# Gated linear attention into an FFN on one core: the FFN's activation, the weights' low parts and the order of the program rewritten

## The chip, the cores and the metric

One core of a Trainium2 chip runs the whole program in one launch. The metric is the device time of an execution in microseconds (us). The engines of a core run side by side, each in the order of its own queue: PE (TensorE, matrix products into PSUM banks), DVE (VectorE), ACT (ScalarE), POOL (GpSimd) and SP (SyncE, which here only issues DMAs). They wait for each other by semaphores.

## What is computed

```python
for t in range(S):                                   # B=4, H=8, S=768, D=48
    state = alpha[:, :, t, :, None] * state + einsum('bhd,bhe->bhde', k[:, :, t], v[:, :, t])
    y[:, :, t] = einsum('bhd,bhde->bhe', q[:, :, t], state)
x = y.transpose(0, 2, 1, 3).reshape(3072, 384)
h = x @ w_in                                         # w_in 384 x 2048
g = where(h >= 1, h, where(h <= -1, 0, (h + 1)**2 / 4))
out = (g @ w_out).astype(float32)                    # w_out 2048 x 384
```

The attention's inputs are float32. The weights are float64 (8 bytes a number) in device memory and are turned into fp32 on the chip.

## The kernel before, in words

**Chunks.** The sequence is cut into 24 chunks of 128 tokens, six to a batch entry. `prepare` (lines 452 to 529) loads a chunk and makes its running products of alpha: two scans on DVE (L498 forward, L505 backward, a reciprocal L502 between them), the product with the keys (L513, DVE) and with the queries (L526, POOL). `attend` (777 to 804) turns it: PE transposes (L545), scores (L560) and the state's update (L573), DVE masks the scores (L646) and adds to the state (L600, L602), ACT or POOL copy the state for PE (L592, L595), and PE makes the outputs (L700). `end_chunk` (726 to 774) brings the outputs into the layout of the FFN: for the first three chunks one fp32 copy on ACT (L738); for later ones a rounded part on ACT (L747) and the rest by DVE's subtraction (L752) in a ring, and behind the last chunk of a group six small DMAs of SP (L768) that move pieces between partitions.

**Groups.** Three chunks are a group of 384 tokens, eight groups in all. Each group runs over 16 blocks of 128 columns of w_in ("f-blocks"): a first product (x by w_in) into a PSUM bank h, the activation, a second product (g by w_out) added up in three PSUM banks over the 16 blocks. In group 0 both are plain fp32 products (L819 and L920). From group 1 on each number is split into a rounded high part and a low part and a product is three products of parts, 9 matmuls (L828, "split" first product; L929, split second product). For that g is split too: the high part by ACT (L894), the low part by POOL or DVE (L895). The last f-block's sums are copied by ACT or DVE (L332) and sent out (L968).

**Activation before** (lines 861 to 890): DVE clips h to -1..1 into gf (L876), ACT makes (0.5 gf + 0.5) squared (L861), DVE takes the maximum with h (L887). For f-blocks with a key under CLIPS = 6 (the first five of group 0) ACT makes three operations instead of DVE's clip: Relu(-0.5 h + 0.5) out of PSUM, Relu(1 - that), Square.

**Weights.** Two f-blocks share one tile of w_in and one of w_out ("wt", 128 x 768 float64, 768 KB), 16 tiles in all. `decode` (340 to 399) makes fp32 of a tile: ACT (L350, L358), DVE shift (L366), DVE sign (L377), and an integer addition (L389) that POOL or DVE makes. Group 0 uses the decoded tiles as they are. For group 1 and later, `part_w` (401 to 415) makes the rounded high part on ACT (L404) and the low part by a subtraction on POOL or, as the other way, DVE (L405).

**The order.** Nothing is written in program order: every operation is handed to a `Plan` (75 to 226) with an engine, an assumed time, a key (roughly the time at which it is due) and what it reads and writes. `Plan.order` then goes through the program on the host and puts on each engine's queue, one after the other, what can start soonest by the assumed times, the smallest key first. An operation may name a second engine ("other"), which then counts LATER later. The constants in lines 31 to 51 set the keys: LAG is by how many f-blocks the second product follows the first, FETCH, LOAD, DECODE and PARTED how far ahead the weights are fetched, decoded and split, PREPARE and the MARGINs how far ahead chunks are made ready, MERGE from which chunk on a group's f-blocks are planned together with the next chunk. RATE is the assumed rate of a DMA. Where PE would idle for long at the beginning, matmuls of zeros are put in ("fills", L980).

Of the kernel before, what the change touches and what calls it, by code (L numbers as in the profile page):

```python
# [14 lines left out]
AF = mybir.ActivationFunctionType  # L15
ALU = mybir.AluOpType
# [14 lines left out]
LAG = 3.0  # L31
FETCH = 12.0
LOAD = 6.0
DECODE = 3.0
PARTED = 6.0
PREPARE = 2.5
MARGIN = 11.0
MARGIN0 = 9.0
MARGIN1 = 6.0
FETCH0 = 18.0  # L40
DECODE0 = 4.0
AHEAD = 20.0
FIRST = 5
ROOM = 2
LATER = 4.0
MERGE = 6
WARMTH = 60.0
HELP = 4
QFAST = 3
CLIPS = 6.0  # L50
# [24 lines left out]
class Plan:  # L75
# [6 lines left out]
    ISSUE, LAND, RATE = 0.42, 1.9, 190e3  # L82
# [50 lines left out]
    def order(self):  # L133
        free = {"PE": 1.0, "DVE": 1.0, "ACT": 1.0, "POOL": 5.0, "SP": 1.0}
# [95 lines left out]
def gated_attention_ffn(ctx: ExitStack, tc: tile.TileContext, q, k, v, alpha, w_in, w_out, by, out):  # L230
    nc = tc.nc
# [20 lines left out]
        out=mask, in_=mask, compare_op=ALU.is_ge, fill=0.0, base=0, pattern=[[1, P]], channel_multiplier=-1  # L252
# [53 lines left out]
    with ExitStack() as main:  # L306
# [33 lines left out]
        def decode(u, which, raw, key):  # L340
# [7 lines left out]
                0.88,  # L348
# [7 lines left out]
                0.87,  # L356
# [35 lines left out]
                1.82,  # L392
# [414 lines left out]
        def hidden(n, f, key):  # L807
# [57 lines left out]
            if key < CLIPS:  # L865


                act(h, AF.Relu, -0.5, half_b)
                act(gf, AF.Relu, -1.0, ones)
                act(gf, AF.Square, 1.0, 0.0)  # L870
            else:
                plan.op(
                    "DVE",
                    0.08 + 0.45 * w,
                    key + 0.4,
                    lambda: nc.vector.tensor_scalar(  # L876
                        out=gf(), in0=h(), scalar1=-1.0, scalar2=1.0, op0=ALU.max, op1=ALU.min
                    ),
                    [h],
                    [gf],  # L880
                )
                act(gf, AF.Square, 0.5, half_b)
# [4 lines left out]
                lambda: nc.vector.tensor_tensor(out=gf(), in0=gf(), in1=h(), op=ALU.max),  # L887
# [307 lines left out]
```

## Time and profile before

| | |
|---|---|
| runs | median 545.0 us (544.95 to 545.48, 3 runs) |
| the profiled execution | 543.69 us, of which its span in the trace 541.4 us |
| granted clock of PE, mean | 0.986 |
| PE busy | 517.4 us, 96% |
| DVE, ACT, POOL busy | 381.7, 251.9, 171.8 us: 70%, 47%, 32% |

Shares of busy time are means over the span. The slices of the page show where an engine is full and where it is not; the releaser of an idle time is the instruction whose end let the waiting one start. A duration in a row is that of the instruction on its engine, with what it lost there to others.

### The profile page before, as it was taken

The numbers are of one execution on the slowest core, as the hardware profiler recorded it, in microseconds if no ns is written. First come the engines' busy times: TensorE is split into PE (matmuls) and PEld (weight loads), VectorE is DVE, ScalarE is ACT, GpSimd is POOL, SyncE is SP. The second block draws the span as 40 slices with busy tenths as digits, with TensorE's granted clock in tenths as the row PEclk, the third lists the DMA queues.
The fourth block names the chain that finished last, engine by engine and source line by source line (L and its number), as shares of the span: only waits on it lengthen the run. The fifth ranks groups of instructions, "written<-read, shape, count | busy, mean of one in ns | idle before, by whom it ended". The sixth has DMA issues, their size and how long they took to land.

```text
span 541.4 us, 11717 instructions
## 1 busy us (share of the span) xinstructions
PE 517.4 (96%) x4753; PEld 471.5 (87%) x4753; DVE 381.7 (70%) x637; ACT 251.9 (47%) x455; POOL 171.8 (32%) x180
## 2 busy tenths in 40 slices
PE   7998979788999999999999999999999999999996
PEld 5875545456999999999999999999999999999995
DVE  6688988989976587577687677667677656555553
ACT  2578847544444444444444444444444444334331
POOL 5746677666541232042122322133114300000000
PEclk8999998999999999999999999999999999999999
DMA  7998350716421232042123132033202011001001
GB/s 183 281 327 259 124 158 0 234 35 157 126 84 57 50 113 84 16 106 81 49 83 86 39 110 84 16 91 110 78 6 58 21 45 24 1 1 45 0 1 48
DMA packets 22330, 46.98 MB, mean 87 GB/s; under 512 B 3616, under 2 KB 11776, under 8 KB 22272
## 3 DMA queue, kind: packets, MB, share of 16 engines
q1 hardware_dynamic: 22272, 46.18, 29.5%
q8 instruction: 39, 0.64, 0.5%
q14 instruction: 19, 0.16, 0.1%
HBM read 39.38 MB, written 4.72 MB: 81 GB/s over the span
## 4 chain that ended last, share of the span: by engine, by line
PE 86%; DVE 5%; DMA 3%; issue 2%; POOL 2%; SPq 0%; ACT 0%; POOLq 0%; DVEq 0%; ACTq 0%
PE ps L828 33%; PE ps L929 33%; PE ps L700 5%; PE ps L920 4%; PE ps L819 3%; PE ps L573 2%; PE ps L560 2%; PE ps L545 2%; PE ps L980 2%; DMA both<-in_vb 1%; DVE w L377 1%; DVE inv L505 1%; POOL wt L389 1%; DMA wt<-in_w_out 1%; DMA raw_kq<-in_kq 1%
## 5 line engine op out<-in xcount | busy, mean ns | idle before, releaser
L828 PE MATMUL ps<-ring,wt 128*128 128x384 f32 x1008 | 197.4, 340 | 0.0
L929 PE MATMUL ps<-gh,wt 128*128 128x384 f32 x1008 | 197.4, 340 | 0.0
L828 PEld LDWEIGHTS ps<-ring,wt 128*128 128x128 f32 x1008 | 178.0, 188 | 1.1
L929 PEld LDWEIGHTS ps<-gh,wt 128*128 128x128 f32 x1008 | 177.3, 188 | 0.6 <-issue 0.2
L861 ACT ACTIVATE gf<-gf,half_b 128x384 f32<-128x384 f32 x123 | 76.0, 618 | 136.2 <-DVE gf L876 134.9
L887 DVE TENSOR_TENSOR gf<-gf,ps 128x384 f32<-128x384 f32 x128 | 70.3, 550 | 59.4 <-ACT gf L861 58.5
L894 ACT CAST gh<-gf 128x384 fp32r<-128x384 f32 x112 | 57.5, 513 | 72.7 <-DVE gf L887 69.3
L876 DVE TENSOR_SCALAR gf<-ps 128x384 f32<-128x384 f32 x123 | 68.2, 554 | 24.8 <-PE ps L828 18.3
L895 POOL TENSOR_TENSOR gh<-gf,gh 128x384 fp32r<-128x384 f32 x38 | 41.5, 1092 | 103.7 <-ACT gh L894 88.7
L895 DVE TENSOR_TENSOR gh<-gf,gh 128x384 fp32r<-128x384 f32 x74 | 42.8, 578 | 41.8 <-ACT gh L894 41.8
L526 POOL TENSOR_TENSOR Q<-pre,raw_kq 128x512 f32<-128x512 f32 x24 | 31.6, 1315 | 127.4 <-PE ps L700 117.0
L920 PE MATMUL ps<-gf,wt 128*128 128x384 f32 x96 | 37.3, 535 | 6.1 <-POOL wt L389 4.9
L405 POOL TENSOR_TENSOR wt<-wt 128x768 fp32r<-128x768 f32 x15 | 33.6, 2244 | 13.8 <-ACT wt L404 13.6
L920 PEld LDWEIGHTS ps<-gf,wt 128*128 128x128 f32 x96 | 19.7, 212 | 19.1 <-POOL wt L389 5.8
L498 DVE TENSOR_TENSOR_SCAN pre<-raw_a,fwd 128x516 f32<-128x516 f32 x24 | 31.4, 1309 | 5.2 <-POOL fwd L273 2.1
L819 PE MATMUL ps<-wt 128*128 128x384 f32 x96 | 33.0, 491 | 1.9 <-POOL wt L389 1.9
L505 DVE TENSOR_TENSOR_SCAN inv<-raw_a,bwd 128x516 f32<-128x516 f32 x24 | 31.9, 1331 | 0.3
L819 PEld LDWEIGHTS ps<-wt 128*128 128x128 f32 x96 | 18.5, 196 | 14.2 <-POOL wt L389 2.8
L592 ACT COPY both<-state 48x192 f32<-48x192 f32 x69 | 24.0, 348 | 11.7 <-POOL state L677 5.3
L548 ACT COPY ks<-ps 128x512 f32<-128x512 f32 x24 | 14.1, 588 | 28.8 <-PE ps L545 28.7
L700 PE MATMUL ps<-other,both 128*64 128x64 f32 x372 | 27.0, 226 | 0.0
L700 PE MATMUL ps<-Q,both 128*64 128x64 f32 x372 | 26.9, 226 | 0.0
(69 smaller groups left out, 494.6 us busy)
## 6 DMA issues: line engine op xcount, KB each, us to landing
raw_kq<-in_kq SPq DMA_DIRECT2D x48, 192.0 KB, 3.8
raw_a<-in_al SPq DMA_DIRECT2D x24, 258.5 KB, 2.6
both<-in_vb SPq DMA_DIRECT2D x48, 128.0 KB, 2.8
wt<-in_w_in SPq DMA_DIRECT2D x8, 768.0 KB, 8.8
wt<-in_w_out SPq DMA_DIRECT2D x8, 768.0 KB, 5.4
vt<-in_vt SPq DMA_DIRECT2D x24, 192.0 KB, 3.2
out<-ot SPq DMA_DIRECT2D x24, 192.0 KB, 1.9
ring<-ring SPq DMA_DIRECT2D x42, 48.0 KB, 2.2
```

Of the source, the lines that this page charges most:

```text
L405: sub = lambda e: e.tensor_tensor(out=part(1), in0=data(), in1=part(0).bitcast(F32), op=ALU.subtract)
L505: lambda: nc.vector.tensor_tensor_scan(flat(inv())[:, ::-1], a[:, 1 : n + 1][:, ::-1], flat(bwd)[:, ::-1], 0.0, ALU.mult, ALU.max),
L700: nc.tensor.matmul(out=ps()[halves[r], to, halves[u]], lhsT=lhsT[:, u, r], rhs=x()[:, g, halves[u]], start=m + u == 0, stop=True, skip_gro ...
L819: nc.tensor.matmul(out=h(), lhsT=raw_in(f)[:, kt], rhs=whole_x(n)()[:, kt].rearrange("p j t -> p (j t)"), start=kt == 0, stop=kt == KT - 1,)
L828: nc.tensor.matmul(out=h(), lhsT=win(f, w)[:, kt], rhs=ring[:, at, kt, a, :], start=(m == 0), stop=(m == 3 * KT - 1),)
L861: lambda: nc.scalar.activation(out=gf(), in_=in_(), func=func, scale=scale, bias=bias),
L876: lambda: nc.vector.tensor_scalar(out=gf(), in0=h(), scalar1=-1.0, scalar2=1.0, op0=ALU.max, op1=ALU.min),
L887: lambda: nc.vector.tensor_tensor(out=gf(), in0=gf(), in1=h(), op=ALU.max),
L894: plan.op("ACT", 0.08 + 0.41 * w, key + 0.4, lambda: nc.scalar.copy(out=gh()[:, 0], in_=gf()), [gf], [gh])
L895: sub = lambda e: e.tensor_tensor(out=gh()[:, 1], in0=gf(), in1=gh()[:, 0].bitcast(F32), op=ALU.subtract)
L920: nc.tensor.matmul(out=o_ps[seg][m](), lhsT=raw_out(f)[:, m * P : (m + 1) * P], rhs=gh(), start=f == f0, stop=f == f1 - 1,)
L929: nc.tensor.matmul(out=o_ps[seg][m](), lhsT=wout(f, w)[:, m * P : (m + 1) * P], rhs=gh()[:, a], start=(f == f0 and i == 0), stop=(f == f1 ...
```

## The change

The activation becomes two operations on ACT, r = Relu(0.5 h + 0.5) out of PSUM and r squared, and one on DVE, max(min(r squared, 1), h), for all f-blocks alike; the clip on DVE (L876), the maximum (L887) and the three-operation form go, and CLIPS with them. The low part of the weights is made by DVE alone. The constants of the plan, some of its assumed times, its assumed DMA rate and the engines' assumed first free times are others, so the order is made anew on all engines. Line numbers of the new file are smaller by one to 25.

```diff
-LAG = 3.0   FETCH = 12.0  LOAD = 6.0   DECODE = 3.0   PARTED = 6.0   PREPARE = 2.5
-MARGIN = 11.0  MARGIN0 = 9.0  MARGIN1 = 6.0  FETCH0 = 18.0  DECODE0 = 4.0  AHEAD = 20.0
-FIRST = 5   ROOM = 2  LATER = 4.0  MERGE = 6  HELP = 4  QFAST = 3  CLIPS = 6.0
+LAG = 5     FETCH = 9     LOAD = 11.0  DECODE = 12.5  PARTED = 10.5  PREPARE = 3.5
+MARGIN = 9.0   MARGIN0 = 9.5  MARGIN1 = 5.5  FETCH0 = 22    DECODE0 = 2.0  AHEAD = 8
+FIRST = 4   ROOM = 3  LATER = 5.0  MERGE = 3  HELP = 7  QFAST = 16
-    ISSUE, LAND, RATE = 0.42, 1.9, 190e3
+    ISSUE, LAND, RATE = 0.42, 1.9, 280e3
-        free = {"PE": 1.0, "DVE": 1.0, "ACT": 1.0, "POOL": 5.0, "SP": 1.0}
+        free = {"PE": 2.5, "DVE": 2.5, "ACT": 2.5, "POOL": 6.0, "SP": 2.8}
...
-                1.82,
+                1.95,
-                other=("DVE", 1.55, lambda: add(nc.vector), True),
+                other=("DVE", 0.96, lambda: add(nc.vector), True),
...
-            plan.op(
-                "POOL",
-                1.8,
-                key,
-                lambda: sub(nc.gpsimd),
-                [raw, parts],
-                [parts],
-                port=True,
-                other=("DVE", 0.88, lambda: sub(nc.vector), True),
-            )
+            plan.op("DVE", 0.88, key, lambda: sub(nc.vector), [raw, parts], [parts], port=True)
...
-            if key < CLIPS:
-                act(h, AF.Relu, -0.5, half_b)
-                act(gf, AF.Relu, -1.0, ones)
-                act(gf, AF.Square, 1.0, 0.0)
-            else:
-                plan.op("DVE", ..., lambda: nc.vector.tensor_scalar(
-                        out=gf(), in0=h(), scalar1=-1.0, scalar2=1.0, op0=ALU.max, op1=ALU.min), [h], [gf])
-                act(gf, AF.Square, 0.5, half_b)
+            act(h, AF.Relu, 0.5, half_b)
+            act(gf, AF.Square, 1.0, 0.0)
             plan.op("DVE", ...,
-                lambda: nc.vector.tensor_tensor(out=gf(), in0=gf(), in1=h(), op=ALU.max),
+                lambda: nc.vector.scalar_tensor_tensor(
+                    out=gf(), in0=gf(), scalar=1.0, in1=h(), op0=ALU.min, op1=ALU.max),
                 [gf, h], [gf])
```

(The constants are set several to a line here, and three statements are drawn together.)

Counts on the queues, before and after: fills on PE 159 and 98; L876 on DVE 123 and none; the low part of the weights on DVE 1 and 16, on POOL 15 and none; the low part of g on DVE 74 and 86, on POOL 38 and 26; ACT's activations 138 and 256.

**DVE at the start**, behind the product of chunk 0. "pre", "bwd" and "inv" are a chunk's scans, reciprocal and product with the keys; "Q" is masked scores. Before:

```order
L498 SCALAR_TENSOR_TENSOR pre<-raw_a,fwd 128x516
L646 TENSOR_TENSOR Q<-ps,mask 64x4x64 x2
L600 COPY state<-ps 128x192
L502 RECIPROCAL bwd<-pre 128x4
L602 TENSOR_TENSOR state<-state,ps 128x192
L505 SCALAR_TENSOR_TENSOR inv<-raw_a,bwd 128x516
L513 TENSOR_TENSOR inv<-inv,raw_kq 128x4x128
L646 TENSOR_TENSOR Q<-ps,mask 64x4x64 x2
```

and with the change (L488, L492, L495, L503 are the lines that were L498, L502, L505, L513; L636, L590 and L592 were L646, L600 and L602):

```order
L488 SCALAR_TENSOR_TENSOR pre<-raw_a,fwd 128x516
L492 RECIPROCAL bwd<-pre 128x4
L495 SCALAR_TENSOR_TENSOR inv<-raw_a,bwd 128x516
L503 TENSOR_TENSOR inv<-inv,raw_kq 128x4x128
L636 TENSOR_TENSOR Q<-ps,mask 64x4x64 x2
L590 COPY state<-ps 128x192
L592 TENSOR_TENSOR state<-state,ps 128x192
L636 TENSOR_TENSOR Q<-ps,mask 64x4x64 x2
```

Chunk 1's scans, reciprocal and product now stand in one piece behind chunk 0's, and the masks of chunk 0 behind them.

**POOL while the weights of group 0 are decoded.** L389 is the addition of the decode, L405 the low part of a weight tile, L526 the product with the queries. Before:

```order
L405 TENSOR_TENSOR wt<-wt 128x768
L389 TENSOR_TENSOR wt<-w,wt 128x768
L595 COPY both<-state 48x4x48
L389 TENSOR_TENSOR wt<-w,wt 128x768
L405 TENSOR_TENSOR wt<-wt 128x768 x2
L389 TENSOR_TENSOR wt<-w,wt 128x768 x2
L405 TENSOR_TENSOR wt<-wt 128x768 x2
L526 TENSOR_TENSOR Q<-pre,raw_kq 128x512
L521 COPY meet<-inv 128x4
L389 TENSOR_TENSOR wt<-w,wt 128x768
```

and with the change (L388 is the addition, L585 a copy of the state, L618 a mask by selection, L667 the state's decay, L516 the product with the queries):

```order
L388 TENSOR_TENSOR wt<-w,wt 128x768
L585 COPY both<-state 48x4x48 x2
L388 TENSOR_TENSOR wt<-w,wt 128x768
L618 AFFINE_SELECT other<-other 64x512
L667 TENSOR_TENSOR state<-state,pre 128x192
L585 COPY both<-state 48x4x48 x2
L388 TENSOR_TENSOR wt<-w,wt 128x768
L516 TENSOR_TENSOR Q<-pre,raw_kq 128x512
L511 COPY meet<-inv 128x4
L388 TENSOR_TENSOR wt<-w,wt 128x768 x3
L585 COPY both<-state 48x4x48 x2
L618 AFFINE_SELECT other<-other 64x512
```

The low parts are gone from POOL; small operations of the chunks stand between the additions.

**DVE from chunk 5's ring copy on**, with the change: L742 is the ring copy (L752 before), L404 the low part of a weight tile, L861 the new operation of the activation.

```order
L742 TENSOR_TENSOR ring<-ps,ring 128x4x128
L592 TENSOR_TENSOR state<-state,ps 128x192
L861 SCALAR_TENSOR_TENSOR gf<-gf,ps 128x384
L404 TENSOR_TENSOR wt<-wt 128x768
L495 SCALAR_TENSOR_TENSOR inv<-raw_a,bwd 128x516
L503 TENSOR_TENSOR inv<-inv,raw_kq 128x4x128
L404 TENSOR_TENSOR wt<-wt 128x768
L861 SCALAR_TENSOR_TENSOR gf<-gf,ps 128x384
L404 TENSOR_TENSOR wt<-wt 128x768 x2
L488 SCALAR_TENSOR_TENSOR pre<-raw_a,fwd 128x516
L404 TENSOR_TENSOR wt<-wt 128x768
L861 SCALAR_TENSOR_TENSOR gf<-gf,ps 128x384 x2
```

Here five low parts follow within eleven instructions of the ring copy; before, DVE had one in the whole program, ahead of its ring copy of chunk 5.

## Rows read from the trace of the kernel before

**Rows 1.** The page: busy time in us, share of the span and instructions of each engine.

```profile
PE 517.4 (96%) x4753; PEld 471.5 (87%) x4753; DVE 381.7 (70%) x637; ACT 251.9 (47%) x455; POOL 171.8 (32%) x180
```

**Rows 2.** Windows, by stage. Columns: from:to and length in us, then busy us (and instructions) of PE, PE's weight loads, DVE, ACT, POOL, then PE's granted clock, the busy share of the DMA engines and GB/s.

```profile
0.00:37.30 37.30, 32.66 (x508) 26.57 (x508) 25.96 (x34) 18.26 (x34) 20.78 (x35) 0.95 0.89 251
37.30:121.00 83.70, 71.38 (x520) 43.55 (x520) 74.34 (x91) 54.83 (x83) 59.05 (x37) 0.94 0.46 146
121.00:140.00 19.00, 16.89 (x159) 12.79 (x158) 17.86 (x31) 10.17 (x20) 13.50 (x10) 1.00 0.57 152
140.00:500.00 360.00, 360.00 (x3367) 352.87 (x3366) 243.70 (x448) 156.18 (x298) 78.45 (x99) 1.00 0.22 61
```

**Rows 3.** Timeline of PE from 119 to 129 us: start, us, engine, line, operation, tiles, in brackets the idle time before it and what ended it.

```profile
121.55 2.10 PE L819 MATMUL ps<-wt 128*128 128x384 f32 x6
123.48 2.10 PE L920 MATMUL ps<-gf,wt 128*128 128x384 f32 x6
127.69 0.66 PE L545 MATMUL ps<-ident,inv 128*128 128x128 f32 x4 [2.11 <-DVE inv L513]
128.10 1.13 PE L828 MATMUL ps<-ring,wt 128*128 128x384 f32 x5
```

**Rows 4.** Waits of PE from 37 to 128 us: who waits for whom, us in total, times, the longest.

```profile
PE ps L545 <- DVE inv L513: 6.0, 3, 3.0
```

**Rows 5.** The chain of waits that ended last, its pieces around the first split product: start, us, what.

```profile
112.78 2.48 DVE w L377
...
120.27 0.70 DVE ring L752
...
120.99 0.74 SPq L768
...
123.07 1.96 DMA ring<-ring
...
125.07 1.72 DVE inv L505
```

**Rows 6.** Source views of single lines, whole span: duration in ns min/median/max, first and last start in us, shape.

```profile
L366 DVE TENSOR_SCALAR w<-w x16: 547/726/2199, 27.1 to 128.0; 128x768 int32<-128x768 int32 x16
...
L377 DVE SCALAR_TENSOR_TENSOR w<-wt,w x16: 942/959/2480, 27.7 to 129.8; 128x768 int32<-128x768 int32 x16
...
L498 DVE TENSOR_TENSOR_SCAN pre<-raw_a,fwd x24: 1221/1233/2877, 5.3 to 411.5; 128x516 f32<-128x516 f32 x24
...
L405 DVE TENSOR_TENSOR wt<-wt x1: 2417/2417/2417, 67.9 to 67.9; 128x768 fp32r<-128x768 f32 x1
```

**Rows 7.** Groups of POOL from 37.3 to 121 us: line, engine, operation, tiles, count | busy us, mean ns | idle time before and what ended it.

```profile
L405 POOL TENSOR_TENSOR wt<-wt 128x768 fp32r<-128x768 f32 x12 | 27.6, 2302 | 10.3 <-ACT wt L404 10.2
L389 POOL TENSOR_TENSOR wt<-w,wt 128x768 int32<-128x768 int32 x10 | 20.3, 2028 | 9.2 <-DVE w L377 5.4 <-DVE gf L887 1.9 <-issue 1.0
L526 POOL TENSOR_TENSOR Q<-pre,raw_kq 128x512 f32<-128x512 f32 x4 | 6.1, 1525 | 0.0
```

**Rows 8.** Groups of DVE from 37.3 to 121 us, same columns.

```profile
L377 DVE SCALAR_TENSOR_TENSOR w<-wt,w 128x768 int32<-128x768 int32 x13 | 15.6, 1203 | 0.3
L366 DVE TENSOR_SCALAR w<-w 128x768 int32<-128x768 int32 x13 | 13.7, 1055 | 0.5 <-ACT w L350 0.3
...
L498 DVE TENSOR_TENSOR_SCAN pre<-raw_a,fwd 128x516 f32<-128x516 f32 x4 | 6.5, 1638 | 0.0
L505 DVE TENSOR_TENSOR_SCAN inv<-raw_a,bwd 128x516 f32<-128x516 f32 x4 | 6.5, 1616 | 0.0
L876 DVE TENSOR_SCALAR gf<-ps 128x384 f32<-128x384 f32 x10 | 5.5, 549 | 2.9 <-PE ps L819 1.6 <-PE ps L920 1.2
L389 DVE CUSTOM_DVE_ANT_0 wt<-wt,w 128x1536 uint16<-128x1536 uint16 x3 | 5.1, 1706 | 0.1
L513 DVE TENSOR_TENSOR inv<-inv,raw_kq 128x512 f32<-128x512 f32 x4 | 5.0, 1260 | 0.1
...
L677 DVE TENSOR_TENSOR state<-state,pre 128x192 f32<-128x192 f32 x1 | 1.6, 1601 | 0.0
```

**Rows 9.** Source views of the activation's operations on ACT, whole span (ns min/median/max), and the page's group of the low part on POOL (busy us, mean ns).

```profile
L861 ACT ACTIVATE gf<-gf,half_b x123: 597/618/622, 60.7 to 531.9; 128x384 f32<-128x384 f32 x123
...
L861 ACT ACTIVATE gf<-ps,half_b x5: 563/581/582, 39.5 to 56.5; 128x384 f32<-128x384 f32 x5
...
L861 ACT ACTIVATE gf<-gf x5: 522/523/524, 40.8 to 57.7; 128x384 f32<-128x384 f32 x5
...
L895 POOL TENSOR_TENSOR gh<-gf,gh 128x384 fp32r<-128x384 f32 x38 | 41.5, 1092 | 103.7 <-ACT gh L894 88.7
```

**Rows 10.** Timeline of DVE at the start.

```profile
10.94 1.23 DVE L498 TENSOR_TENSOR_SCAN pre<-raw_a,fwd 128x516 f32<-128x516 f32 x1 [1.46 <-DMA raw_a<-in_al]
...
15.78 1.05 DVE L513 TENSOR_TENSOR inv<-inv,raw_kq 128x512 f32<-128x512 f32 x1
20.89 0.88 DVE L646 TENSOR_TENSOR Q<-ps,mask 64x256 f32<-64x256 f32 x2 [4.06 <-PE ps L573]
```

**Rows 11.** Timeline of SP at the start (a DMA's issue), and the page's row of w_in's loads (count, KB each, median us from issue to landing).

```profile
19.90 0.42 SPq L432 DMA_DIRECT2D wt<-in_w_in  x1
...
wt<-in_w_in SPq DMA_DIRECT2D x8, 768.0 KB, 8.8
```

**Rows 12.** Window of 6 us (columns as in rows 2).

```profile
80.00:86.00 6.00, 5.04 (x34) 2.59 (x32) 4.36 (x10) 4.14 (x6) 4.45 (x4) 0.54 0.11 28
```

More of the change, by code (lines that the diff above doesn't have):

```diff
@@ L30 @@
 WARM = 20
[L31 to L50, printed above, removed]
+LAG = 5
+FETCH = 9
+LOAD = 11.0
+DECODE = 12.5
+PARTED = 10.5
+PREPARE = 3.5
+MARGIN = 9.0
+MARGIN0 = 9.5
+MARGIN1 = 5.5
+FETCH0 = 22
+DECODE0 = 2.0
+AHEAD = 8
+FIRST = 4
+ROOM = 3
+LATER = 5.0
+MERGE = 3
+WARMTH = 60
+HELP = 7
+QFAST = 16
 NEAR = 0.0
@@ L347, in decode @@
                 "ACT",
-                0.88,
+                0.91,
                 key,
@@ L355, in decode @@
                 "ACT",
-                0.87,
+                0.91,
                 key,
@@ L403, in part_w @@
             data = lambda: word(raw(), F32, 1)
-            plan.op("ACT", 0.8, key, lambda: nc.scalar.copy(out=part(0), in_=data()), [raw], [parts])
+            plan.op("ACT", 0.9, key, lambda: nc.scalar.copy(out=part(0), in_=data()), [raw], [parts])
             sub = lambda e: e.tensor_tensor(out=part(1), in0=data(), in1=part(0).bitcast(F32), op=ALU.subtract)
-            plan.op(
-                "POOL",
-                1.8,
-                key,
-                lambda: sub(nc.gpsimd),
-                [raw, parts],
-                [parts],
-                port=True,
-                other=("DVE", 0.88, lambda: sub(nc.vector), True),
-            )
+            plan.op("DVE", 0.88, key, lambda: sub(nc.vector), [raw, parts], [parts], port=True)
         raws_w = {}
@@ L864, in hidden @@
             )
-            if key < CLIPS:
-                act(h, AF.Relu, -0.5, half_b)
-                act(gf, AF.Relu, -1.0, ones)
-                act(gf, AF.Square, 1.0, 0.0)
-            else:
[L872 to L881, printed above, removed]
-                act(gf, AF.Square, 0.5, half_b)
+            act(h, AF.Relu, 0.5, half_b)
+            act(gf, AF.Square, 1.0, 0.0)
             plan.op(
@@ L886, in hidden @@
                 key + 0.4,
-                lambda: nc.vector.tensor_tensor(out=gf(), in0=gf(), in1=h(), op=ALU.max),
+                lambda: nc.vector.scalar_tensor_tensor(
+                    out=gf(), in0=gf(), scalar=1.0, in1=h(), op0=ALU.min, op1=ALU.max
+                ),
                 [gf, h],
```

## Prediction, made before the changed kernel ran

> **What bounds the kernel now.** I read the page's busy shares first [rows 1]: TensorE (PE) is busy 96% of the span, so the question is where the missing 4% lies. The table by stage [rows 2] answers it: from 140 to 500 us PE is busy for all of 360.00 us, and nothing that VectorE (DVE), ScalarE (ACT) or GpSimd (POOL) does faster there can shorten the run. What can be won lies before the first split product, which starts at 128.10 [rows 3]. Up to 37.3 PE holds mostly fills, from there to 121 it idles 83.70 − 71.38 = 12.3 us, and it idles 2.11 us more just before 128.10. Its longest wait there is for a chunk's product on DVE, 6.0 us in three times [rows 4]. In the same 83.7 us DVE idles only some 4.2 us by its rows (its 91 instructions last 79.5 us; overlaps at their ends make 74.34 in the table), and the chain of waits runs through it: L377, then L752, the ring moves on SP and their DMA, and a scan [rows 5], whose product PE waits for [rows 3]. So **DVE sets when group 1 can begin**, and the forecast is a sum over DVE's queue.
>
> Part of DVE's time is not work but stretch. L366 takes 547 ns at best and up to 2199, L377 942 and up to 2480, the scans 1221 and up to 2877 [rows 6], in a stretch in which POOL runs 27.6 + 20.3 + 6.1 = 54.0 us of large two-input operations [rows 7]. Against the short durations (.55, .96, 1.23, .68 and .43 us) the groups of [rows 8] hold this stretch: L366 13.7 − 13 × .55 = 6.55; L377 15.6 − 13 × .96 = 3.1; eight scans 13.0 − 8 × 1.23 = 3.2; L389 5.1 − 3 × .96 = 2.2; L513 5.0 − 4 × .68 = 2.3; L405 2.4 − .96 = 1.45; L677 1.6 − .43 = 1.2. Together 20.0 us, so DVE's own work is 59.5.
>
> **The change, part by part.**
>
> *Activation.* Per f-block it takes one DVE operation away (L876, .55 us) and turns ACT's Square with bias (.62) into a Relu out of PSUM (.58) and a plain Square (.52) [rows 9]: DVE −.55, ACT +.48. From 140 us on this is worth nothing, since PE waits for nothing there; ACT, 156.18 of 360 us busy [rows 2], gains about 110 × .48 = 53 us and stays under 60%. The chain from product to second product is still three or four operations, and LAG lets it run five f-blocks ahead where it was three. Before the first split product it takes 10 L876 off DVE (5.5 us [rows 8]); the first five blocks used ACT alone and now use two ACT operations instead of three.
>
> *Low parts.* Twelve L405 (27.6 us) leave POOL in that stretch; DVE had one and now has six before chunk 5's ring copy and ten behind it. No row shows an L405 on DVE beside a quiet POOL: .96 is the median of L377, same tile size, two inputs; 2.42 is the one L405 that DVE has [rows 6]. I take .96 in DVE's own work, plus a share of stretch below.
>
> *Order: start.* Before, chunk 0's masks and state stand between chunk 1's first scan and its second; its product ends at 16.83, and DVE then idles 4.06 us for chunk 1's update [rows 10]. Now chunk 1's scans, reciprocal and product stand in a row from 10.94: 1.23 + .18 + 1.23 + 1.05, end 14.7. The 25 DVE instructions from there to the decode's end and chunk 3's masks cost 16.2 us at short durations and 18.8 at those of 22 to 27 us: 30.9 to 33.5. I take 32.5 for the start of the next piece; a wait like the 4.06 would make it 36. POOL's first L405, which stood ahead of chunk 2's select, is gone from there too. The piece that before starts at 37.3 so starts at 32.5: **−4.8**.
>
> *Order: up to chunk 5's ring copy.* DVE now has 15 L366, 15 L377, 4 L389 and 6 subtractions (8.25 + 14.4 + 3.84 + 5.76), 7 scans and 3 products (8.61 + 2.04), 4 reciprocals, 6 state updates, 8 masks and 3 ring copies (8.3, at the lengths that these have in the same view before) and 14 of the new minimum-maximum operations at L876's .55 (7.7): 58.9 us, against 59.5: **−.6**. An operation with a third input might cost up to L377's .96 instead, scaled to half the elements (.48), so .55 is no low guess.
>
> *Stretch.* POOL keeps 11 L389 and 4 L526 there. At the means of [rows 7] that is 28.4 us. I scale: 20.0 × 28.4 / 54.0 = 10.6, so **−9.4**. Bounds: 0 (stretch unchanged) and −20. The idle 4.2 I keep. Ring copy of chunk 5: 32.5 + 58.9 + 10.6 + 4.2 = 106.2, against 120.96.
>
> The Trainium skill's page "SBUF — State Buffer", section "SBUF: two separate sides", speaks against moving subtractions to DVE: DVE operations with two SBUF inputs and POOL operations take one port pair in turn, and the later one blocks until the first has ended. By that rule, an estimate, one collision adds up to a whole POOL addition, 2.03 us by the mean row, so .96 becomes 2.99; with that price the last rival's sum below would be 115.5 + 17.9 − 128.1 − 1.5 + 15.0 = +18.8, or 563.8 us. The long rows of L377 and the L405 on DVE agree in kind. The sum goes by rows and does without it.
>
> *From there to the first split product.* Before: 120.96 to 128.10, 7.1 us, of which ring moves and DMA 4.1 and the scan and product the rest [rows 3, 5]. Now chunk 6's transposes stand behind two split products, but two and a half whole second products stand ahead. 4.1 to 7.1; I keep 7.1: first split product at **113.3**, −14.8.
>
> *PE's work behind it.* 15 of the 16 second products of group 0 now stand ahead (14 before): −1.93, the distance from 121.55 to 123.48; chunk 7's transposes fall behind: +.4 [rows 3]. **−1.5**.
>
> *DVE in group 1.* Ten subtractions follow. For the second product that PE reaches 21.7 us into group 1, DVE has 22.0 us of own work behind the ring copy, some 4 of stretch, then cast and low part (about .5 as the plain Square, and 1.09 [rows 9]): 27.6 − 7.1 = 20.5, a margin of 1.2. Two of the eight subtractions in it as long as the 2.42 row cost 2 × 1.46 = 2.9, less 1.2: **+1.7**. Bounds 0 and 10 (below).
>
> *Loads.* SP issues chunk inputs ahead of weights; w_in1, issued at 19.90 [rows 11], now stands behind chunk 3's queries, about 26. The decode of it is 16 us later in DVE's queue, w_in takes 8.8 us to land [rows 11], so I cost it at nothing; without that cover it is up to +6.1. Fills fall from 159 to 98, all ahead of the first product. The granted clock was .54 in one stretch, behind an idle PE [rows 12]; one such stretch of 6 us more would be +2.8 at most, and fewer waits work against it, so I take nothing.
>
> **Sum:** −14.8 − 1.5 + 1.7 = −14.6 us, against the profiled execution's 543.69: 529.1. That execution lies 1.3 below the median of the runs, so the forecast is **530.4 us**.
>
> **Rivals.**
>
> *Stretch stays.* If DVE's long instructions come from any POOL work beside them rather than from its amount, 20.0 stays: ring copy 115.6, first split product 122.7, −5.4 − 1.5 + 1.7 = −5.2, **539.8**. For it: a long row, as the L377 of 112.78 [rows 5], may need only one POOL operation beside it, and 15 are left. Against: twelve subtractions of 2.3 us are half of POOL's time, and fewer of them can meet fewer instructions of DVE.
>
> *PE becomes the bound.* No idle time once it starts: 128.1 − 6.4 (start at 30.9) − 12.3 − 2.1 − 2.0 (chunk 3's turn now ahead of the first product) = 105.3, and −1.5: −24.3, **520.7**. Against: DVE's 58.9 us hardly leave room, and weights still arrive through DVE and POOL in turn.
>
> *Loads late:* +6.1, **536.5**.
>
> *Subtractions blocked, slower.* DVE holds all 16, in queue order, each beside a POOL addition, at price p. With the other stretch as before (18.55), the first split product is at 32.5 + 53.1 + 18.55 + 4.2 + 7.1 + 6p = 115.5 + 6p, and group 1 stalls by 8 × (p − .96) − 1.2. It breaks even at p of about 1.6; at 2.42, the one row there is, it is +1.9 − 1.5 + 10.5 = +10.9, **555.9**. For it: that row. Against: POOL has little left once its 11 additions are done, and the ten later subtractions meet mostly single ones.
>
> **How the numbers follow.** Forecast .50 (525 to 536 by the start's and the stretch's bounds); stretch stays .20; PE the bound .12; loads late .05; blocked near break-even, so no change, .04; blocked fully .09. About .2% (1.1 us) is what a measurement can tell from nothing. Faster .87, same .04, slower .09. The range takes in the forecast, both cases next to it and most of the PE-bound one: 520 to 541.
>
> **What the changed profile would show.** Right: first whole product near 33 to 34, first split product near 113, L366 and L377 groups before it nearer .75 and 1.05 than 1.06 and 1.20 us, the new L404 rows on DVE near 1 to 1.5 us, and a PE that is busy without a gap from about 140 on. Wrong: L404 rows of 2 us or more, PE waiting for low parts in group 1, weights that land after DVE asks for them, or ACT as what ends PE's and DVE's waits, with 73.7 us for at least 55 us of ACT work.

## The result, and the profile after

The changed kernel takes 522.25 us (median of 4 runs, 519.71 to 523.83) where the kernel before took 544.98 in the same runs: a ratio of 0.958, with a 95% interval of 0.954 to 0.962. That is 22.7 us less. The forecast was 14.6 less, 530.4 us, in a range of 520 to 541; the result lies in the range, near its lower end, and 1.6 us from the time of the rival "PE becomes the bound" (520.7).

The profiled execution took 521.67 us with a span of 520.0. Busy times of the page after, which answer to [rows 1]:

```profile
PE 503.3 (97%) x4692; PEld 463.0 (89%) x4692; DVE 327.7 (63%) x529; ACT 308.0 (59%) x578; POOL 134.1 (26%) x163
```

The stages after, to be read against [rows 2]: the first ends behind chunk 3's masks on DVE (in [rows 2] it ends where PE's first whole product begins, which is at 33.99 now), the second with chunk 5's ring copy (columns as there).

```profile
0.00:34.95 34.95, 27.57 (x517) 22.72 (x518) 27.94 (x39) 17.52 (x33) 19.83 (x37) 0.95 0.94 244
34.95:103.70 68.75, 64.06 (x453) 39.70 (x452) 63.66 (x82) 51.60 (x83) 37.84 (x33) 1.00 0.64 203
103.70:140.00 36.30, 36.30 (x358) 32.71 (x357) 34.82 (x51) 28.49 (x54) 20.98 (x21) 1.00 0.37 106
140.00:480.00 340.00, 340.00 (x3170) 333.30 (x3168) 188.01 (x334) 194.76 (x381) 55.40 (x75) 1.00 0.22 59
```

PE now idles 4.7 of 68.75 us in the second stage (12.3 of 83.70 before), its granted clock there is 1.00 (.94 before), and from 103.70 to 480 it is full. DVE is busy 63.66 of the same 68.75 us. The first split product (L818) starts at 108.32 instead of 128.10, as PE's timeline shows (compare [rows 3]); the transposes (L535), which stood ahead of it and waited 2.11 us for DVE, come behind two split products.

```profile
102.81 5.97 PE L896 MATMUL ps<-gf,wt 128*128 128x384 f32 x18
108.32 3.63 PE L818 MATMUL ps<-ring,wt 128*128 128x384 f32 x18
111.78 0.60 PE L535 MATMUL ps<-ident,inv 128*128 128x128 f32 x4
```

DVE's groups in the second stage, to be read against [rows 8]. L376, L365, L404, L488, L388 and L495 were L377, L366, L405, L498, L389 and L505:

```profile
L376 DVE SCALAR_TENSOR_TENSOR w<-wt,w 128x768 int32<-128x768 int32 x14 | 15.2, 1087 | 0.4
L365 DVE TENSOR_SCALAR w<-w 128x768 int32<-128x768 int32 x14 | 14.8, 1059 | 3.1 <-ACT w L349 2.6 <-POOL both L585 0.3
...
L404 DVE TENSOR_TENSOR wt<-wt 128x768 fp32r<-128x768 f32 x6 | 6.7, 1134 | 0.0
L488 DVE TENSOR_TENSOR_SCAN pre<-raw_a,fwd 128x516 f32<-128x516 f32 x4 | 5.0, 1258 | 0.0
L388 DVE CUSTOM_DVE_ANT_0 wt<-wt,w 128x1536 uint16<-128x1536 uint16 x4 | 4.5, 1116 | 0.0
L495 DVE TENSOR_TENSOR_SCAN inv<-raw_a,bwd 128x516 f32<-128x516 f32 x3 | 3.7, 1226 | 0.0
...
L503 DVE TENSOR_TENSOR inv<-inv,raw_kq 128x512 f32<-128x512 f32 x3 | 2.1, 688 | 0.1
```

and POOL's there, against [rows 7]:

```profile
L388 POOL TENSOR_TENSOR wt<-w,wt 128x768 int32<-128x768 int32 x10 | 19.8, 1984 | 20.1 <-DVE w L376 14.4 <-ACT gf L851 1.6 <-ACT other L608 1.5
L516 POOL TENSOR_TENSOR Q<-pre,raw_kq 128x512 f32<-128x512 f32 x4 | 5.9, 1480 | 1.4 <-DVE pre L488 1.2
```

L365 is as long on the mean as before (1.06 us, where the prediction's own sign was a mean nearer .75), but the scans, the products and the additions are short again. Against the short durations of the prediction the stretch is 7.1 (L365) + 1.8 (L376) + .9 (L404) + .7 (L388) + .1 (scans) = 10.6 us, which is what was forecast, beside 25.7 us of POOL's large two-input operations (L388 and L516). All low parts, on DVE, as the source view gives them (ns min/median/max):

```profile
L404 DVE TENSOR_TENSOR wt<-wt x16: 929/993/1766, 58.4 to 129.2; 128x768 fp32r<-128x768 f32 x16
```

PE's longest waits from 30 to 140 us:

```profile
PE ps L896 <- DVE wt L388: 1.6, 1, 1.6
PE ps L563 <- ACT ks L538: 1.3, 1, 1.3
PE ps L896 <- POOL wt L388: 0.8, 1, 0.8
```

Before, beside the 6.0 us for DVE's products [rows 4], the same view from 37 to 128 us had two rows for POOL's addition of the decode, together 6.8 us:

```profile
PE ps L920 <- POOL wt L389: 4.9, 3, 3.0
PE ps L819 <- POOL wt L389: 1.9, 2, 1.4
```

### The profile page after: what moved, and what is told of

The parts are those of the page before. It is cut to its first block, busy times and chain, and to the rows that moved or that the text cites. A ratio compares the mean times of both kernels' runs of the same rounds, so it can differ in the third digit from the quotient of the medians.

```text
span 520.0 us, 11664 instructions
## 1 busy us (share of the span) xinstructions
PE 503.3 (97%) x4692; PEld 463.0 (89%) x4692; DVE 327.7 (63%) x529; ACT 308.0 (59%) x578; POOL 134.1 (26%) x163
## 4 chain that ended last, share of the span: by engine, by line
PE 81%; DMA 6%; DVE 5%; issue 3%; ACT 2%; POOL 1%; SPq 1%; DVEq 0%; ACTq 0%; POOLq 0%
PE ps L818 35%; PE ps L905 34%; PE ps L690 4%; DMA wt<-in_w_in 3%; PE ps L896 2%; PE ps L563 2%; DMA raw_a<-in_al 2%; PE ps L550 2%; DMA vt<-in_vt 1%; PE ps L535 1%; DVE w L365 1%; DVE pre L488 1%; ACT w L349 1%; DVE w L376 1%; DVE wt L388 1%
## 5 line engine op out<-in xcount | busy, mean ns | idle before, releaser
L818 PE MATMUL ps<-ring,wt 128*128 128x384 f32 x1008 | 197.8, 340 | 0.0
L818 PEld LDWEIGHTS ps<-ring,wt 128*128 128x128 f32 x1008 | 178.0, 188 | 1.6
L861 DVE SCALAR_TENSOR_TENSOR gf<-gf,ps 128x384 f32<-128x384 f32 x128 | 70.1, 549 | 126.8 <-ACT gf L851 126.6
L851 ACT ACTIVATE gf<-ps,half_b 128x384 f32<-128x384 f32 x128 | 74.3, 580 | 111.3 <-PE ps L818 98.4
L516 POOL TENSOR_TENSOR Q<-pre,raw_kq 128x512 f32<-128x512 f32 x24 | 30.2, 1258 | 160.4 <-PE ps L690 151.7
L871 DVE TENSOR_TENSOR gh<-gf,gh 128x384 fp32r<-128x384 f32 x86 | 48.0, 558 | 35.4 <-ACT gh L870 35.3
L851 ACT ACTIVATE gf<-gf 128x384 f32<-128x384 f32 x128 | 67.3, 526 | 3.8
L871 POOL TENSOR_TENSOR gh<-gf,gh 128x384 fp32r<-128x384 f32 x26 | 32.3, 1245 | 64.5 <-ACT gh L870 61.9
L896 PE MATMUL ps<-gf,wt 128*128 128x384 f32 x96 | 33.6, 492 | 2.7 <-DVE wt L388 1.6
L809 PE MATMUL ps<-wt 128*128 128x384 f32 x96 | 33.2, 490 | 1.2 <-issue 0.7
L488 DVE TENSOR_TENSOR_SCAN pre<-raw_a,fwd 128x516 f32<-128x516 f32 x24 | 29.7, 1238 | 4.1 <-POOL fwd L272 2.1
L896 PEld LDWEIGHTS ps<-gf,wt 128*128 128x128 f32 x96 | 18.1, 196 | 14.7 <-DVE wt L388 2.9
L495 DVE TENSOR_TENSOR_SCAN inv<-raw_a,bwd 128x516 f32<-128x516 f32 x24 | 30.7, 1278 | 0.6
L388 POOL TENSOR_TENSOR wt<-w,wt 128x768 int32<-128x768 int32 x11 | 21.7, 1972 | 20.1 <-DVE w L376 14.4
L690 PEld LDWEIGHTS ps<-Q,both 128*64 128x64 f32 x372 | 24.0, 140 | 1.9 <-issue 0.4
L503 DVE TENSOR_TENSOR inv<-inv,raw_kq 128x512 f32<-128x512 f32 x24 | 25.2, 1050 | 0.2
```

Of the source, the lines that this page charges most:

```text
L488: lambda: nc.vector.tensor_tensor_scan(flat(pre()), a[:, 0:n], flat(fwd), 0.0, ALU.mult, ALU.max),
L495: lambda: nc.vector.tensor_tensor_scan(flat(inv())[:, ::-1], a[:, 1 : n + 1][:, ::-1], flat(bwd)[:, ::-1], 0.0, ALU.mult, ALU.max),
L516: mul = lambda e: e.tensor_tensor(out=Q(), in0=pre()[:, :, 1:], in1=raw_kq[:, i, 1], op=ALU.mult)
L690: nc.tensor.matmul(out=ps()[halves[r], to, halves[u]], lhsT=lhsT[:, u, r], rhs=x()[:, g, halves[u]], start=m + u == 0, stop=True, skip_gro ...
L809: nc.tensor.matmul(out=h(), lhsT=raw_in(f)[:, kt], rhs=whole_x(n)()[:, kt].rearrange("p j t -> p (j t)"), start=kt == 0, stop=kt == KT - 1,)
L818: nc.tensor.matmul(out=h(), lhsT=win(f, w)[:, kt], rhs=ring[:, at, kt, a, :], start=(m == 0), stop=(m == 3 * KT - 1),)
```

## The experiments

The change has three parts: the activation, the low parts on DVE, and the constants with the order that follows from them. The plan makes the order anew for each kernel, so an edit of one part also moves other work, and the constants were not chosen again for any of these kernels. All six partial combinations were run, then five edits of the changed kernel and one that joins two of them. Each had four or more runs beside runs of the kernel before. The letters of the theories are explained where each first stands in an expectation.

**The new activation alone.** The constants, assumed times and low parts of before; on DVE the one operation of the change takes the place of clip and maximum:

```diff
-            if key < CLIPS: ...
+            act(h, AF.Relu, 0.5, half_b)
+            act(gf, AF.Square, 1.0, 0.0)
```

> The kernel before with the new activation alone; constants, assumed times and low parts on POOL or DVE as before. Theory D (DVE's queue up to chunk 5's ring copy sets the time: its own work plus a stretch of some .4 us for each us of large POOL operations): DVE's own work there falls by 1 us net (10 clips gone, but four low parts and two more additions land on DVE), 12 low parts stay on POOL, so the stretch stays near 19: 541 to 544 us. Theory O (the constants, that is the rebuilt order, carry nearly all of the gain): 545 within .5. Theory A (the activation carries it): under 535.

547.51 us, ratio 1.005 (1.003 to 1.007): 2.6 us slower, outside all three. DVE's own work fell by 1.5 us, but chunk 5's ring copy came .8 us later and the first split product 2.5 later. The stretch was 21.6 us beside 40.8 us of large POOL operations, where it had been 20.0 beside 54.0: less work on POOL, and no less stretch. That speaks against scaling the stretch by POOL's amount. In this order PE waited 7.9 us for DVE's chunk products (6.0 before), so the instructions saved on DVE gained nothing.

**The low parts on DVE alone** (with ACT's cast of a weight tile assumed to take .9 us instead of .8).

```diff
-            plan.op("POOL", 1.8, key, lambda: sub(nc.gpsimd), ..., other=("DVE", 0.88, ...))
+            plan.op("DVE", 0.88, key, lambda: sub(nc.vector), [raw, parts], [parts], port=True)
```

> The kernel before with the low parts on DVE alone. D: own work of DVE +4, stretch -10 (POOL keeps 9 additions there), start as before: 536 to 540 us if group 1 does not wait for the nine later subtractions. O: 545 within .5. Theory B (each subtraction on DVE is blocked by a POOL operation, 2.4 us apiece): 550 or more, with the subtraction's mean above 2 us.

555.03 us, ratio 1.019 (1.017 to 1.021). The time is that of theory B, but not its mechanism: the six subtractions ahead of the ring copy took 1.16 us on the mean, not 2.4, the stretch fell from 20 to 5.0 us and chunk 5's ring copy came 9 us earlier, at 111.9, as D has it. The loss came behind the ring copy, in PE's order:

```profile
114.36 0.66 PE L536 MATMUL ps<-ident,inv 128*128 128x128 f32 x4 [1.69 <-DVE inv L504]
...
128.33 6.56 PE L810 MATMUL ps<-wt 128*128 128x384 f32 x12 [4.74 <-DVE wt L389]
134.44 1.87 PE L819 MATMUL ps<-ring,wt 128*128 128x384 f32 x8
```

Two turns of chunks and the whole products of the last weight tile were put ahead of the first split product, these waiting 4.74 us for a weight that DVE decoded late: 22.5 us from the ring copy to the first split product instead of 7.1, and 5.3 us more from there to the end.

**The constants alone.**

> The old activation and low parts on POOL or DVE with the changed kernel's constants, assumed times and DMA rate. D: DVE's own work +2, POOL now has 14 additions and all 16 low parts (some 65 us of large operations), so a stretch of 20 to 25; the start is better by 3 to 5: 538 to 544 us. O: 522 to 527 us.

538.89 us, ratio .989 (.987 to .991): D. The order brought the first whole product to 33.85 and the way from ring copy to first split product to 4.0 us, but 14 low parts and 14 additions on POOL, 57.4 us, beside DVE made its instructions longer than before:

```profile
L377 DVE SCALAR_TENSOR_TENSOR w<-wt,w 128x768 int32<-128x768 int32 x15 | 25.5, 1698 | 0.4
L366 DVE TENSOR_SCALAR w<-w 128x768 int32<-128x768 int32 x14 | 22.0, 1575 | 0.3 <-ACT w L350 0.3
```

```profile
L405 POOL TENSOR_TENSOR wt<-wt 128x768 fp32r<-128x768 f32 x14 | 28.7, 2051 | 4.2 <-ACT wt L404 3.9
L389 POOL TENSOR_TENSOR wt<-w,wt 128x768 int32<-128x768 int32 x14 | 28.7, 2050 | 12.6 <-DVE w L377 5.5 <-ACT gf L861 3.1 <-ACT w L350 2.5
```

The stretch was 34 us and the ring copy later than before (123.9). The better order paid for a longer DVE.

**Activation and low parts, constants of before.**

> New activation and low parts on DVE with the constants of before. D: DVE's own work +8 (13 low parts now stand ahead of chunk 5's ring copy), stretch -9, start as before: 541 to 546 us. O: 545 within .5. Theory A: under 535.

538.52 us, ratio .989 (.985 to .992), better than D and worse than A: DVE's own work rose by some 7 us, the stretch fell to 10.3, the ring copy was at 118.0, and PE's work behind the first split product was 1.6 us shorter.

**Activation and constants, low parts on POOL or DVE.**

> New activation and new constants, low parts on POOL or DVE as before. With the constants alone DVE ran 58.6 us of own work with 34 us of stretch beside 63.6 us of large POOL operations. D: own work 3 to 4 less (11 clips gone, three low parts more), POOL 4 us less, so 2 us less stretch: 532 to 535 us. O: 522 to 527.

535.74 us, ratio .983 (.980 to .986): .7 above D's range and far from O. The stretch was 34.8 us.

**Low parts and constants, activation of before.**

> Old activation, low parts on DVE, new constants. D: against the changed kernel DVE has nine clips more, one addition more and one low part fewer ahead of chunk 5's ring copy, +4 to +5, at the same stretch of 10 to 11: 525 to 528 us. O: 522 within 1. Theory B (subtractions blocked): 535 or more.

529.86 us, ratio .972 (.968 to .976), 2 us above D's range; the ring copy was at 109.4 (103.7 with the activation too), the stretch 7.4.

Together, in us (median):

| activation | low parts | constants | time | against before | chunk 5's ring copy, first split product |
|---|---|---|---|---|---|
| old | old | old | 545.0 | | 121.0, 128.1 |
| new | old | old | 547.5 | +2.6 | 121.8, 130.6 |
| old | new | old | 555.0 | +10.1 | 111.9, 134.4 |
| old | old | new | 538.9 | −6.1 | 123.9, 127.9 |
| new | new | old | 538.5 | −6.4 | 118.0, 125.0 |
| new | old | new | 535.7 | −8.8 | 121.9, 126.6 |
| old | new | new | 529.9 | −14.7 | 109.4, 113.2 |
| new | new | new | 522.25 | −22.7 | 103.7, 108.3 |

No part carries the gain. From the changed kernel, taking the constants back costs 16.3 us, the low parts 13.5, the activation 7.6: 37 together, where the gain is 22.7; the single parts add up to +6.6. The constants gain in every company, 6.1 us alone and 25.2 beside the low parts; the activation and the low parts cost time alone, and each gains beside any other part. Why they do was read from the traces and not tested by itself, since the order changed with every part.

**More work on POOL.** The changed kernel, with

```diff
+            for c in range(3):
+                cut = slice(256 * c, 256 * c + 256)
+                plan.op("POOL", 0.01, key, lambda cut=cut: nc.gpsimd.tensor_tensor(out=scratch,
+                    in0=data()[:, cut], in1=part(0)[:, cut].bitcast(F32), op=ALU.subtract), [raw, parts], [])
```

> The changed kernel with an extra subtraction of each weight tile on POOL, in three pieces of 256 columns into a scratch tile that nobody reads (some 2 us a tile; six tiles before chunk 5's ring copy), the queues of PE, DVE and ACT unchanged up to there. D: 12 us more of POOL work there at .4 us of stretch each give +5: 526 to 529 us, with DVE's long instructions longer. Theory P (PE is the bound from its first whole product on; DVE has room): 523 or less, as stretch is absorbed.

547.18 us: 18 us above D's range, but its mechanism shows ahead of the ring copy. Up to the ring copy, where the queues of DVE, PE and ACT were the same but for two neighbours on DVE, POOL had 19.3 us more, and DVE's stretch rose from 10.6 to 17.0 us, .33 us for each us of the extra work:

```profile
L377 DVE SCALAR_TENSOR_TENSOR w<-wt,w 128x768 int32<-128x768 int32 x14 | 16.9, 1204 | 0.4
L366 DVE TENSOR_SCALAR w<-w 128x768 int32<-128x768 int32 x14 | 16.1, 1148 | 2.8 <-ACT w L350 2.7
L405 DVE TENSOR_TENSOR wt<-wt 128x768 fp32r<-128x768 f32 x6 | 9.3, 1559 | 0.0
```

```profile
L389 POOL TENSOR_TENSOR wt<-w,wt 128x768 int32<-128x768 int32 x11 | 22.4, 2032 | 11.7 <-DVE w L377 6.0 <-ACT gf L858 1.6 <-ACT other L615 1.5
L409 POOL TENSOR_TENSOR scratch<-wt 128x256 f32<-128x256 f32 x18 | 19.3, 1070 | 1.1
```

and the ring copy came at 113.6, 9.9 us later: 6.4 of stretch, and the rest nearly all in one wait of 3.8 us at a mask (L643), for which the profile shows no releaser. The other 15 us of the loss came in group 1, where the extra operations, now 29 in 40 us, stood in POOL's queue ahead of other work:

```profile
ACT wt L404 <- POOL scratch L409: 11.7, 4, 4.0
...
PE ps L570 <- ACT ks L545: 10.0, 2, 5.6
```

ACT waited for the scratch operations and PE for ACT. That wait is the experiment's own.

**The additions on DVE too.**

```diff
-            plan.op("POOL", 1.95, key, lambda: add(nc.gpsimd), ..., other=("DVE", 0.96, ...))
+            plan.op("DVE", 0.96, key, lambda: add(nc.vector), [w, raw, (u, which)], [raw], port=True)
```

> The changed kernel with the decode's integer addition on DVE alone, so that POOL keeps no weight work. D: DVE's own work up to chunk 5's ring copy +8.3 (85.0 for 76.7 us from chunk 1's first scan on), stretch -7 to -9: 521 to 524 us, so no gain that can be told. If stretch does not come from POOL's additions: 529 or more. P: 518 to 521, as PE's waits for weights shrink.

525.37 us, ratio .963 (.961 to .966), 1.4 above D's range. L365 fell to .58 us with POOL's additions gone, and 11 more additions cost .96 each:

```profile
L376 DVE SCALAR_TENSOR_TENSOR w<-wt,w 128x768 int32<-128x768 int32 x14 | 15.3, 1090 | 0.5
L388 DVE CUSTOM_DVE_ANT_0 wt<-wt,w 128x1536 uint16<-128x1536 uint16 x15 | 14.4, 960 | 1.8
L365 DVE TENSOR_SCALAR w<-w 128x768 int32<-128x768 int32 x14 | 8.1, 577 | 1.9 <-ACT w L349 1.7
```

From the first whole product to the ring copy it took 70.2 us as against 69.7. The stretch fell from 10.6 to 3.0 us, so ten additions on POOL had cost DVE some .76 us each, about four fifths of what one takes on DVE itself. The order changed too: the first whole product came 2.2 us later than in the changed kernel, which is most of the 3.1 us that this kernel is behind it.

**DVE relieved.** The changed kernel without `decode`'s `plan.op("DVE", 0.52, ...)`, the shift of L365; it leaves out a step that the weights need.

> The changed kernel without DVE's shift in the decode of the weights (16 instructions left out, so the weights' exponents are wrong). D: 14 of them stood ahead of chunk 5's ring copy and took 14.8 us with their stretch; DVE's queue there falls from 76.7 to 67.8 us of own work: 509 to 514 us. P (from its first whole product on PE is the bound): PE idles 4.7 us between its first whole product and chunk 5's ring copy, so 517.5 at the lowest.

519.73 us, ratio .954 (.951 to .956): P, above its lowest time of 517.5 and 6 us above D's range. The ring copy came 8 us earlier (95.7), but PE is full:

```profile
35.65:95.70 60.05, 58.06 (x442) 36.97 (x441) 55.65 (x69) 50.09 (x83) 31.78 (x26) 1.00 0.75 232
95.70:103.00 7.30, 7.30 (x26) 4.40 (x24) 7.12 (x12) 6.33 (x13) 2.11 (x4) 1.00 0.46 115
```

The first split product came at 103.0, and 415.3 us remained behind it (411.7 in the changed kernel). The stretch hardly fell, from 10.6 to 9.9 us: with the shift gone, the sign (L365 in this kernel) is what meets POOL's additions, and it takes 1.58 us on the mean for .96.

```profile
L365 DVE SCALAR_TENSOR_TENSOR w<-wt,w 128x768 int32<-128x768 int32 x14 | 22.1, 1581 | 2.1 <-ACT w L349 1.9
```

**PE relieved.** The last third of each first product of group 0 is left out.

```diff
                     if whole:
+                        if kt == KT - 1:
+                            continue
```

> The changed kernel with two of the three matmuls in each first product of group 0 (the last third of the sum is left out). PE loses 32 of 96 records of some .35 us each, 11 us, all ahead of or around the first split product; DVE's queue is the same up to chunk 5's ring copy. D: 520 to 522 us. P: 511 to 514.

521.94 us, ratio .960 (.956 to .964): D. The first products took 23.3 us instead of 33.2, and the time stayed within the noise of 522.25; PE idles 10 of 70.6 us instead of 4.7 of 68.8, at a granted clock of .95 instead of 1.00, and DVE's stage is as long:

```profile
32.84:103.47 70.63, 60.66 (x431) 37.82 (x432) 65.18 (x85) 52.67 (x85) 39.90 (x34) 0.95 0.64 206
```

**An earlier decode.** `DECODE0 = 4.0` instead of 2.0 in the changed kernel.

> The changed kernel with DECODE0 4.0 instead of 2.0: the sign step of the first weight tile comes ahead of chunk 3's scans, and 72.4 instead of 76.7 us of DVE's own work stand from chunk 1's first scan to chunk 5's ring copy (one pair of scans falls behind it). D: 517 to 520 us. P: 521 to 523, as PE idles only 4.7 us there and the first whole product is not earlier by more than 1.

524.31 us, ratio .963 (.960 to .965): 2.1 us slower than the changed kernel, and 1.3 above P's range. The ring copy came at 100.2, 3.5 us earlier, and the first split product at 108.1, as without the edit, with PE busy all the way between the two (7.87 of 7.87 us): that is what P says, though not its number. Where the 2 us were lost was not traced further; 413.6 us remained behind the first split product instead of 411.7.

**DVE and PE relieved**, the edits of no_shift and less_pe in one kernel.

> Both of the last edits at once: the shift of the decode left out on DVE and a third of each first product of group 0 left out on PE. Alone the first gave 2.5 us and the second nothing. If DVE and PE are each a bound of their own that stand within some 3 us of each other in the changed kernel (theory DP), both together give far more than the sum of the two: 509 to 515 us. If something third (loads, ACT, POOL) sets the time, 518 to 522.

519.96 us, ratio .954 (.952 to .956): theory DP falls. With both relieved, a third thing holds the time at the same place. Waits from 30 to 110 us (who waits for whom, us, times, longest):

```profile
POOL wt L377 <- DMA vt<-in_vt: 5.5, 1, 5.5
...
ACT w L349 <- DMA wt<-in_w_out: 4.6, 1, 4.6
...
PE ps L552 <- ACT ks L527: 4.1, 1, 4.1
```

Inputs that have not landed hold POOL and ACT, and ACT holds PE. One of these stops can be followed to PE: ACT's queue stood until 85.57 for a load of w_out, so its copy of `ks` (L527) came at 89.06, and PE stood still for 4.1 us until 89.70. Behind that stop PE's granted clock fell, to .50 from 90 to 95 us, the lower of its two levels (1.2 GHz):

```profile
80.00:90.00 10.00, 5.92 (x33) 3.48 (x35) 8.42 (x12) 4.98 (x10) 2.91 (x2) 0.91 0.81 222
90.00:100.00 10.00, 10.00 (x114) 7.26 (x107) 7.36 (x13) 7.69 (x14) 4.86 (x4) 0.74 0.34 93
```

So PE's saved work went into idle time (8.9 us from its first whole product to the ring copy, 2.0 in no_shift) and into the clock, and the first split product came at 104.4. Whether an earlier load, or another place of it in ACT's queue, would have given the time back was not tested.

## Why the prediction was right, and what it mis-sized

The direction, the place and the main mechanism were right: nearly all of the gain lies ahead of the first split product, and DVE's queue with its stretch led there. The sum was 6.8 us short, because three of its terms were mis-sized, all to the same side: DVE's idle time, the way from ring copy to first split product, and group 1 behind it. By the trace (us; the forecast's terms, then what they measured, with the start of DVE's piece taken at 34.98):

| step | forecast | measured |
|---|---|---|
| start of DVE's piece | −4.8 | −2.3 |
| DVE's own work to the ring copy | −.6 | −2.9 |
| stretch | −9.4 | −9.4 |
| DVE's idle time | 0 | −2.7 |
| ring copy to first split product | 0 | −2.5 |
| PE's work behind it, and waits in group 1 | +.2 | −1.6 |
| span | −14.6 | −21.4 |

**Start and own work.** These two errors are one, and cancel. Chunk 1 went as forecast, its product ending at 14.7. DVE's timeline goes on:

```profile
13.20 1.48 DVE L503 TENSOR_TENSOR inv<-inv,raw_kq 128x512 f32<-128x512 f32 x1
...
31.64 0.95 DVE L388 CUSTOM_DVE_ANT_0 wt<-wt,w 128x1536 uint16<-128x1536 uint16 x1
32.51 0.55 DVE L365 TENSOR_SCALAR w<-w 128x768 int32<-128x768 int32 x1
33.09 0.96 DVE L376 SCALAR_TENSOR_TENSOR w<-wt,w 128x768 int32<-128x768 int32 x1
34.09 0.86 DVE L636 TENSOR_TENSOR Q<-ps,mask 64x256 f32<-64x256 f32 x2
```

The addition that ends this decode is done at 32.5, the time that I took. A shift, a sign and two masks (2.4 us) follow up to 34.98; I counted them into the piece, and in the table they stand ahead of it. Of DVE's 67.2 us in the piece 10.6 are stretch, which leaves 56.6, and with those four instructions 59.0, where 58.9 was forecast. That 32.5 was met is luck in part: waits for chunk 2's alpha (.91), for POOL (.58) and for PE (.49) lie ahead of it, which the sum had not counted one by one.

**Stretch.** Right to a tenth, and tested: extra work on POOL raised it (pool_doubled), additions taken off POOL lowered it (adds_on_dve), and with the low parts left on POOL under the new constants it was three times as long. The exact number is luck. The ratio is no constant: .2 to .6 us for each us of large POOL operations, .8 in adds_on_dve, and act_only went the other way. Nor did the stretch go where a scaling would take it from: the shift kept all of its own (6.55 us before, 7.1 now), while the scans, the chunk products, the additions and the subtraction lost most of theirs. `Plan` itself counts the decode's operations on DVE and POOL as shutting each other out (`port=True`), so each new order also changes how often they meet. "Stretch stays" is refuted by the changed kernel itself (10.6), and by parts_only (5.0) and adds_on_dve (3.0).

**Idle time.** I kept 4.2 us, the length of the stretch less that of DVE's instructions; 1.5 remained. The waits in DVE's groups are longer than that, since ends of instructions overlap: 9.1 us before and 4.9 after. The 2.9 us at the clip [rows 8] went with the clip, the waits at the maximum and at the masks fell by 1.5 each, and those at the shift, mostly for ACT, rose by 2.6. I should have asked which of the waits the change takes away.

**Ring copy to first split product.** 7.1 was kept out of 4.1 to 7.1; it was 4.6. The order showed that the transposes had moved behind the split products. What remained was PE's own queue: PE is busy without a gap from the ring copy to the first split product, with the 18 records of whole products that start at 102.81. In less_pe, with less of that work, the way was 3.1 us. I should have taken a value near the lower bound.

**Group 1.** The +1.7 did not come: PE has no idle time from 103.70 to 140. Two subtractions as long as the 2.42 row were assumed; ahead of the ring copy the mean is 1.13, over all 16 the median is .99 and the longest 1.77.

**POOL's queue,** which the sum left out. [rows 4] is the longest single row of PE's waits; POOL's additions held PE for longer, 6.8 us in five waits. Before, seven of the ten additions in the stage began within .6 us of the end of a sign, so DVE's queue stands behind most of that. Three began 1.7 to 3.2 us after it, at 50.88, 64.52 and 87.12, each behind a low part in POOL's own queue; in the changed kernel every addition on POOL ahead of the ring copy begins within .4 us of a sign's end. Moving the low parts therefore helped by a second way, and no run separates it from the stretch.

**The rivals.** "Subtractions blocked" needed 1.6 us apiece and is refuted for this kernel by the same row. A single collision can be seen, though: POOL's addition of 58.61 ends at 61.07, and DVE's shift, begun at 59.26, ends .4 us later with a length of 2.22, where it takes .55 alone.

```profile
58.39 0.95 DVE L404 TENSOR_TENSOR wt<-wt 128x768 fp32r<-128x768 f32 x1
59.26 2.22 DVE L365 TENSOR_SCALAR w<-w 128x768 int32<-128x768 int32 x1
```

```profile
58.61 2.46 POOL L388 TENSOR_TENSOR wt<-w,wt 128x768 int32<-128x768 int32 x1 [1.55 <-DVE w L376]
```

That is how the Trainium skill's page "SBUF — State Buffer", section "SBUF: two separate sides", has it, the later one waiting for the earlier one's end. The section says it of DVE operations with two SBUF inputs or in a two-port mode, which `tensor_scalar`, the shift's operation, can enter under conditions; whether the shift ran in that mode no run here shows. What the rule does not say is how often: POOL's 10 additions cost DVE 7.6 us (10.6 of stretch, 3.0 in adds_on_dve), not ten times the 1.98 that one takes. "PE becomes the bound" was given .12 and a time of 520.7; it came nearer than the forecast. It is half right: less_pe shows that PE alone is not the bound, no_shift that DVE alone is not, and the two together that something third stands there too. At 520 us the kernel has several bounds within 3 us of each other, and which of the loads, ACT and POOL is the third stays open. My sum went over one queue and so could not show this.

**PE's clock** was costed at nothing for the fills; it went the other way. The whole second products took 535 ns on the mean before in the page's group of L920, and now, at a granted clock of 1.00,

```profile
L896 PE MATMUL ps<-gf,wt 128*128 128x384 f32 x90 | 31.4, 492 | 2.7 <-DVE wt L388 1.6 <-POOL wt L388 0.8 <-DMA both<-in_vb 0.2
```

The median is 486 ns in both kernels; before, some records took up to 1008 ns, now none over 599. The whole first products are unchanged (491 and 490 ns). Before, PE stood still for 3.0 us at 74.8 and for 1.0 at 80.2, and from 80 to 86 its granted clock was .54, near the lower of its two levels (1.2 GHz) [rows 12]; now its longest wait in the stage is 1.6 us. That is 3.7 us less of PE's work for 96 records (37.3 to 33.6 us).

## What to carry to other kernels

Where one engine's queue sets the time, count its instructions at their short lengths first, and ask whose doing the rest is: an experiment that adds work to the suspected engine shows it. Do not expect the rest to scale with that engine's work, since the order decides how often the two meet. Before adding up gains on one queue, work out the time at which the next engine would be full; the answer lies at the later of the two, and a gain on one alone ends there. Parts of a change that rest on one order must be measured together: alone, two of these three cost time.

## What the runs showed of the hardware that was not expected

In the changed kernel DVE's longest stretch was not in the two-input operations but in the shift with one input (L365, .55 us alone, 1.06 on the mean beside POOL's additions, .58 without them). It often follows a sign step, whose end starts POOL's addition; in no_shift, without the shift, the next sign took the stretch instead (1.58 us for .96). An int32 addition of 128 x 768 costs 1.85 us on POOL and .96 on DVE, and on POOL it takes another .7 to .8 us of DVE's time in this order. With fewer waits PE's granted clock in the stage was 1.00 instead of .94; the whole second products, some of which had run at the lower clock, became 8% shorter on the mean, and the whole first products did not change.
